# Shifting the queries by one position in a chunked gated linear attention with a feed-forward part

## The chip, the cores and the metric

One core of one Trainium2 chip runs the whole kernel. The metric is the device time of one execution in microseconds (us). The kernel before took 702.83 us in the median of 4 runs beside the changed kernel (702.4 to 703.86). All runs that are told here were of the fast state.

## The reference, cut to what matters

```python
# 4 batches, 8 heads, 768 tokens, head size 48; f = sigmoid(f_logit)
for t in range(S):
    state = f[:, :, t, :, None] * state + einsum('bhd,bhe->bhde', k[:, :, t], v[:, :, t])
    y[:, :, t] = einsum('bhd,bhde->bhe', q[:, :, t], state)
x = y.transpose(0, 2, 1, 3).reshape(3072, 384)
h = x @ w_in                                    # 384 -> 2048
out = (h * sigmoid(1.702 * h)) @ w_out          # 2048 -> 384
```

So a query at t sees its own key ungated, an older key at s through the gates s+1 to t, and whatever came before its chunk through the state.

## The kernel before

Everything is fp32; the weights arrive as 64-bit floats and are converted on VectorE in chains of integer and float operations, all in the first units. The tokens are cut into 12 units of 256 (three for each batch). Within a chunk of 64 tokens the attention is built from six levels: at level l, blocks of 2^l even keys meet the 2^l odd queries that follow them. After each level the odd halves of q and k are multiplied in place by the products of gates ("promote"), so that scores are always plain products. Units 0 to 2 run level by level ("fill"); units 3 to 11 run two levels in one stretch ("V"), and the matmuls of the feed-forward part of an earlier unit are put between the stretches in a fixed order.

```python
X = const.tile([P, 4, NA], F32, name="X")        # q, gated q, k, gated q of the other parity

def begin_q():                                   # gating of q
    nc.vector.tensor_tensor(X[:, J], X[:, 0], F, ALU.mult)

@part("W")
def _():                                         # level 0 and half of the diagonal: 128 columns
    order_v(n + 1)
    sc = scores()
    score(sc.rearrange("p h (a t) -> p h a t", a=NP), lambda h, x: X[rows(h), 2, x:x + G:2],
          lambda h, x: view(X, x, [[J * NA + 1, 2], [2, 64]])[rows(h)])
    promote(0)
    t["A"] = evacuate(512, [(0, 0)])             # scores x mask, 1024 wide

@part("W" if n < N_FILL else "V")
def _():                                         # odd keys x ungated odd queries, and level 1
    ...
    score(s4[:, 0], lambda h, x: X[rows(h), 2, x + 1:x + G:2], lambda h, x: X[rows(h), 0, x + 1:x + G:2])
    score(s4[:, 1], keys(1), tokens(J, LEV[1], 1))
    add(0, ..., start=True)                      # even values into all tokens: 128 columns
    promote(1, True); promote(2)
    t["A"] = evacuate(512, [(0, 0), (256, 1)])

def levels(l):                                   # two more stretches of two levels
    ...

# later: k transposed back (tkn), states st = st * gates + k v^T, then
py += st[c - 1] x X[J]                           # "inter": state of the chunk before x gated q
```

(Cut; `...` marks what is left out.) The tiles in the profile: sc is the PSUM tile of scores (also used for the sums k v^T), A the masked scores, y the PSUM output of the attention, Kc and Qc packed copies of even keys and odd queries, vl the values in the order of a level, st the states, tot the products of gates on GpSimd, bits, a and s the steps of the weights' conversion, h, sg, g and o the feed-forward part, yT and xT its input.

Of the kernel before, what the change touches and what calls it, by code (L numbers as in the profile page):

```python
# [13 lines left out]
ALU = mybir.AluOpType  # L14
# [9 lines left out]
def kernel(  # L24
# [9 lines left out]
):  # L34

# [82 lines left out]
    for u in range(2, NL + 1):  # L118
        nc.gpsimd.tensor_copy(
            perm[:, u - 2].rearrange("p (n m) -> p n m", m=LEV[u - 1]),  # L120
            ident.rearrange("p (n two m) -> p two n m", two=2, m=LEV[u - 1])[:, 0],
        )
# [3 lines left out]


    X = const.tile([P, 4, NA], F32, name="X")
# [107 lines left out]
    V_HALF = [(1, 0), (1, 1)] + [(m, 0) for m in LEV[1:]]  # L236
    NV = len(V_HALF)

# [32 lines left out]
    def load_vl(n, u):  # L271


        if n >= NALL:
            return
        if n < N_TURN:
            for i, x in enumerate((0, 1) if u == 0 else (u,)):
                pt = ps.tile([P, DM], F32, tag="mm", name=f"tv_{n}_{x}", bufs=4)
                for g in range(NG):
                    nc.tensor.matmul(  # L280
                        pt[g * 64:(g + 1) * 64], lhsT=ident[:, x::2] if u == 0 else perm[:, u - 2, :], rhs=vns[n][:, g, :],
                        start=True, stop=True,
                    )
                if i == 0:
                    t = ld.tile([P, 2, DM] if u == 0 else [P, DM], F32, tag=f"vl{u}", name=f"vl_{n}_{u}")
                vls[n, x] = t[:, x] if u == 0 else t
                nc.scalar.copy(vls[n, x], pt)
            return
        v_tok = v_toks[n % 2]
        if u == 0:  # L290
            t = ld.tile([P, 2, DM], F32, tag="vl0", name=f"vl_{n}_0")
            nc.sync.dma_start(out=t, in_=v_tok.rearrange("(p two) e -> p two e", two=2))
            vls[n, 0], vls[n, 1] = t[:, 0], t[:, 1]
        else:
            m, half = V_HALF[u]
            t = vls[n, u] = ld.tile([P, DM], F32, tag=f"vl{u}", name=f"vl_{n}_{u}")
            nc.sync.dma_start(out=t, in_=v_tok.rearrange("(n two m) e -> two n m e", two=2, m=m)[half])
# [22 lines left out]
    def attention(n):  # L320
# [4 lines left out]
        J = 1 if n < N_FILL or (n - N_FILL) % 2 else 3  # L325
        t = {}
# [32 lines left out]
        def begin():  # L359
            turn(1, X[:, 0])  # L360
            if n:
                load_raw(n + 1, 1)

        def begin_k():
            turn(2, X[:, 2])
            if n:
                load_raw(n + 1, 2)

        def begin_gates():
            t["tot"] = att.tile([P, NA], F32, tag="tot", name=f"tot_{n}")  # L370
            t["tms"], off = [F], 0
            for m in LEV:
                nb = NA // (2 * m)
                t2 = t["tms"][-1].rearrange("p (n two) -> p n two", two=2)
                tn = t["tot"][:, off:off + nb]
                nc.gpsimd.tensor_tensor(tn, t2[:, :, 0], t2[:, :, 1], ALU.mult)  # L376
                t["tms"].append(tn)
                off += nb

        def begin_q():  # L380
            nc.vector.tensor_tensor(X[:, J], X[:, 0], F, ALU.mult)
# [13 lines left out]
        def keys(l, tag="Kc"):  # L395
            return lambda h, x: t[tag, l][rows(h), x // 2:x // 2 + 64]
# [20 lines left out]

        def promote(l, q_too=False):

# [4 lines left out]
            qk = view(X, J * NA + m, [[(2 - J) * NA - m, 2], [2 * m, nb], [1, m]])  # L424
# [6 lines left out]
            if l + 1 < NL:  # L431
                m = LEV[l + 1]
                for tag, j, hf in (("Kc", 2, 0), ("Qc", J, 1))[:1 + q_too]:
                    c = t[tag, l + 1] = att.tile([P, NA // 2], F32, tag=tag, name=f"{tag}_{n}_{l}", bufs=2)
                    nc.scalar.copy(  # L435
                        c.rearrange("p (n m) -> p n m", m=m),
                        X[:, j].rearrange("p (n two m) -> p n two m", two=2, m=m)[:, :, hf, :],
                    )
# [17 lines left out]
        @part("W")  # L456
        def _():
            order_v(n + 1)
            sc = scores()
            score(  # L460
                sc.rearrange("p h (a t) -> p h a t", a=NP), lambda h, x: X[rows(h), 2, x:x + G:2],
                lambda h, x: view(X, x, [[J * NA + 1, 2], [2, 64]])[rows(h)],
            )
            promote(0)
            t["A"] = evacuate(512, [(0, 0)])

        @part("W" if n < N_FILL else "V")
        def _():
            sc = scores()
            s4 = sc.rearrange("p h (s a t) -> p s h a t", s=2, a=NP)  # L470
            score(s4[:, 0], lambda h, x: X[rows(h), 2, x + 1:x + G:2], lambda h, x: X[rows(h), 0, x + 1:x + G:2])
            score(s4[:, 1], keys(1), tokens(J, LEV[1], 1))
            A = t["A"]
            t["py"] = ps.tile([P, NG, NP, G], F32, tag="y", name=f"y_{n}")
            add(
                0, lambda h, g, a: A[g * 64:(g + 1) * 64, h, a * G:(a + 1) * G].rearrange("p (two n) -> p n two", two=2),
                lambda h, g, a: t["py"][columns(h, g), g, a, :], start=True,
            )
            if n < N_FILL:
                promote(1)  # L480
            else:
                promote(1, True)
                promote(2)
            t["A"] = evacuate(512, [(0, 0), (256, 1)])

        def level(l):
            sc = scores()
            score(sc[:, :, :256].rearrange("p h (a t) -> p h a t", a=NP), keys(l), tokens(J, LEV[l], 1))
            if l == 2:
                add(1, slot(t["A"], 0), half(1, 1))  # L490
                add(2, slot(t["A"], 256), half(LEV[1], 1))
            else:
                add(l, slot(t["A"], 0), half(LEV[l - 1], 1))
            if n + 1 >= N_TURN:
                for u in (0, 2) if l == 2 else (l,):
                    load_vl(n + 1, u)
            promote(l)
            t["A"] = evacuate(256, [(0, l)])

        def levels(l):  # L500
# [4 lines left out]
            for u, c in ((l - 1, 0), (l, 256)):  # L505
                add(u, slot(t["A"], c), half(LEV[max(u - 1, 0)], 1))
            for u in ((0, 2) if l == 2 else (l - 1, l)):
                load_vl(n + 1, u)
# [5 lines left out]
        if n < N_FILL:  # L514
            for l in range(2, NL):
                part("W")(lambda l=l: level(l))
        else:
            for l in range(2, NL, 2):
                part("V")(lambda l=l: levels(l))

        def turn_k(a0):
# [3 lines left out]
            for a in range(2):  # L525
                for g in range(NG):
                    x = (a0 + a) * U + g * G
                    nc.tensor.transpose(pt[:, a, g, :], X[:, 2, x:x + G], ident)  # L528
# [6 lines left out]
        def _():  # L535
            if n >= N_FILL:
                add(NL - 1, slot(t["A"], 0), half(LEV[-2], 1))
                load_vl(n + 1, NL - 1)
            add(NL, slot(t["A"], 0 if n < N_FILL else 256), half(LEV[-1], 1))
            if n + 1 >= N_TURN:  # L540
                load_vl(n + 1, NL)
# [17 lines left out]
            prev = last.get("st")  # L559
# [13 lines left out]
        def _():  # L573
# [4 lines left out]
            for cs in ((1, 2), (3, 0)):  # L578
                for a in range(NP):
                    for c in cs:  # L580
                        if t["before"][c] is None:
                            continue
                        for h in range(2):
                            x = a * U + c * C
                            nc.tensor.matmul(  # L585
                                py[columns(h, c // 2), c // 2, a, c % 2 * C:(c % 2 + 1) * C],
                                lhsT=t["before"][c][rows(h), a], rhs=X[rows(h), J, x:x + C],
                                start=False, stop=True, skip_group_check=True,
                            )
            yT = att.tile([P, NP, NG, G], F32, tag="kn", name=f"yT_{n}", bufs=1)  # L590
            xT = xTs[n] = mlp.tile([P, NK, U], F32, tag="xT", name=f"xT_{n}", bufs=3)
            for g in range(NG):
                for h in range(2):
                    nc.scalar.copy(yT[rows(h), :, g, :], py[columns(h, g), g])  # L594
            for h in range(2):
                nc.sync.dma_start(
                    out=xT[h * D:(h + 1) * D].rearrange("p c (g t) -> p c g t", g=NG), in_=yT[rows(h), :NK]
                )
                at = 0
                while at < D:  # L600
# [3 lines left out]
                        out=xT[D2 + p:D2 + p + w, c].rearrange("p (g t) -> p g t", g=NG),  # L604
                        in_=yT[h * HS + at:h * HS + at + w, NK],
# [3 lines left out]
        return (begin_f, begin, begin_k, begin_gates, begin_q), parts  # L609


    xTs = {}

    def mlp_h(n, ffs, g):
        t = {}

        def one(ff, c):
            if c == 0:
                if ff % FG == 0:
                    g[ff // FG] = mlp.tile([P, FG, U], F32, tag="g", name=f"g_{n}_{ff}", bufs=6)  # L620
                t["ph"] = ps.tile([P, U], F32, tag="mm", name=f"h_{n}_{ff}", bufs=4)
# [4 lines left out]
            if c == NK - 1:  # L626
                sg = mlp.tile([P, U], F32, tag="sg", name=f"sg_{n}_{ff}")
                nc.scalar.activation(sg, ph, AF.Sigmoid, scale=1.702)  # L628
                nc.vector.tensor_tensor(g[ff // FG][:, ff % FG, :], ph, sg, ALU.mult)  # L629
        return [(U, lambda ff=ff, c=c: one(ff, c), ff // FG * NPC + ff % FG + 1) for ff in ffs for c in range(NK)]  # L630
# [16 lines left out]
    def store(n, tt, o):  # L647
        r0 = n * U + tt * P
# [168 lines left out]
```

## Time and profile before

| | before |
|---|---|
| median, 4 runs | 702.83 us |
| span of the profiled run | 699.6 us |
| TensorE (PE) busy | 677.3 us |
| VectorE (DVE) busy | 397.6 us |
| granted clock, 40 to 60 us | 0.83 (1.00 in the other stretches) |
| period of a steady unit (start of one inter group to the next) | 53.33 us |

The prediction below shows the page's busy shares, the TensorE groups by shape, and a steady unit. One more view is needed for the comparison: what TensorE waited for in the kernel before (who waited for whom: us in all, times, longest).

```profile
PE sc L387 <- DVE A L411: 6.6, 4, 3.1
PE t L346 <- DMA raw<-in_f_logit_dram: 4.4, 1, 4.4
PE o L639 <- DVE g L629: 2.3, 1, 2.3
```

Of the 22 us that TensorE is idle in the whole span, 17.5 are waits in the first 100 us, most of them for VectorE; 1.3 lie between 120 and 220 us, and 3.5 are the end, after the last matmul. So, as an estimate from these waits, a TensorE instruction that goes is worth its whole distance to the next one after about 100 us, and nothing where TensorE stands waiting for VectorE anyway.

### The profile page before, as it was taken

Reading aid. Unit: us, or ns where it says so; the run is one execution under the profiler, and the core shown is the slowest. Engines: PE = TensorE matmul, PEld = TensorE weight load, DVE = VectorE, ACT = ScalarE, POOL = GpSimd, SP = SyncE. Lnnn points to the kernel's source line nnn. Section 1 sums busy time; section 2 is a strip of 40 time slices with the busy share of each in tenths; the row PEclk is TensorE's granted clock in tenths of the full one; section 3 lists DMA queues with packets and bytes.
Section 4 is the critical chain, followed back from the end, with each engine's and each line's share of the span. In section 5 each row is a group of like instructions: output and inputs, shape, how many; then the busy total and the mean of one; then the engine's idle time right before and its main releaser. Section 6 shows DMA issues by size and latency. Waiting matters only on the chain.

```text
span 699.6 us, 20710 instructions
## 1 busy us (share of the span) xinstructions
PE 677.3 (97%) x9208; PEld 507.4 (73%) x9208; DVE 397.6 (57%) x683; ACT 211.7 (30%) x440; POOL 40.6 (6%) x90
## 2 busy tenths in 40 slices
PE   6869989999999999999999999999999999999998
PEld 5647767767776876786786786786786786786774
DVE  4998787986767644644744744744644644441120
ACT  4544433233213322322322322322322332231110
POOL 3020100010002001001001001001001001000000
PEclk9998999999999999999999999999999999999999
DMA  8867963581063615406405405405504202101000
GB/s 205 213 174 185 226 165 103 149 186 37 23 154 102 154 46 144 116 23 151 130 23 145 135 25 144 135 24 138 142 24 113 60 23 65 29 2 36 11 1 22
DMA packets 66898, 69.67 MB, mean 100 GB/s; under 512 B 29944, under 2 KB 59256, under 8 KB 66808
## 3 DMA queue, kind: packets, MB, share of 16 engines
q1 hardware_dynamic: 66808, 68.34, 38.2%
q8 instruction: 72, 1.18, 0.7%
q14 instruction: 18, 0.15, 0.1%
HBM read 58.88 MB, written 8.65 MB: 97 GB/s over the span
## 4 chain that ended last, share of the span: by engine, by line
PE 89%; DVE 6%; DMA 2%; SPq 1%; issue 1%; ACT 1%; DVEq 0%; ACTq 0%
PE o L639 36%; PE h L623 35%; PE sc L387 7%; PE y L445 6%; PE y L585 2%; DMA bits<-in_moe_w_in_dram 1%; PE sc L549 1%; PE tkn L528 1%; DVE s L211 1%; DVE A L411 1%; SPq L246 1%; DVE a L219 1%; DVE X L428 1%; PE t L346 1%; DMA raw<-in_q_dram 1%
## 5 line engine op out<-in xcount | busy, mean ns | idle before, releaser
L623 PE MATMUL h<-xT,w_in 128*128 128x256 f32 x1152 | 262.7, 383 | 0.8 <-DVE g L629 0.8
L639 PE MATMUL o<-w_out,g 128*128 128x384 f32 x768 | 260.7, 491 | 2.3 <-DVE g L629 2.3
L623 PEld LDWEIGHTS h<-xT,w_in 128*128 128x128 f32 x1152 | 216.2, 191 | 36.2 <-issue 2.2
L639 PEld LDWEIGHTS o<-w_out,g 128*128 128x128 f32 x768 | 142.4, 190 | 96.0 <-issue 5.0
L629 DVE TENSOR_TENSOR g<-h,sg 128x256 f32<-128x256 f32 x192 | 80.3, 423 | 143.0 <-ACT sg L628 142.8
L628 ACT ACTIVATE sg<-h 128x256 f32<-128x256 f32 x192 | 72.7, 383 | 177.4 <-PE h L623 167.5
L435 ACT COPY Kc<-X 128x512 f32<-128x512 f32 x60 | 37.7, 629 | 115.0 <-DVE X L430 85.0
L430 DVE TENSOR_TENSOR X<-X,tot 128x1024 f32<-128x1024 f32 x45 | 55.0, 1222 | 19.6 <-PE sc L387 16.2
L411 DVE TENSOR_TENSOR A<-sc,masks 128x512 f32<-128x512 f32 (+1 forms) x84 | 61.1, 756 | 0.0
L445 PE MATMUL y<-A,vl 64*48 64x64 f32 (+1 forms) x2688 | 56.8, 230 | 0.6 <-issue 0.5
L445 PEld LDWEIGHTS y<-A,vl 64*48 64x48 f32 x2688 | 48.9, 121 | 6.1 <-issue 5.8
L334 DVE STREAM_TRANSPOSE X<-raw 128x1024 f32<-128x1024 f32 x18 | 36.9, 2048 | 20.4 <-PE sc L387 14.1
L376 POOL TENSOR_TENSOR tot<-F 128x512 f32<-128x512 f32 x12 | 12.5, 1040 | 544.3 <-DVE st L566 487.5
L658 ACT COPY osb<-o 128x384 f32<-128x384 f32 x18 | 8.6, 478 | 108.8 <-PE o L639 108.7
L594 ACT COPY yT<-y 48x512 f32<-48x512 f32 x48 | 27.8, 580 | 16.6 <-PE y L585 16.0
L387 PE MATMUL sc<-X,Kc 48*64 48x64 f32 x1344 | 28.3, 222 | 2.5 <-DVE A L411 2.5
L387 PEld LDWEIGHTS sc<-X,Kc 48*64 48x64 f32 x1344 | 24.2, 136 | 7.2 <-issue 3.2
L387 PEld LDWEIGHTS sc<-X 48*64 48x64 f32 x768 | 18.6, 138 | 13.8 <-issue 9.3
L569 DVE TENSOR_TENSOR st<-st,sc 128x192 f32<-128x192 f32 x44 | 15.6, 354 | 22.6 <-PE sc L549 21.2
L387 PE MATMUL sc<-X 48*64 48x128 f32 (+1 forms) x768 | 22.9, 254 | 5.5 <-DVE A L411 4.2
L566 DVE TENSOR_TENSOR st<-st,tot 128x192 f32<-128x192 f32 x44 | 15.7, 357 | 20.8 <-PE y L585 11.9
L376 POOL TENSOR_TENSOR tot<-tot 128x256 f32<-128x256 f32 (+4 forms) x60 | 25.8, 431 | 4.7
(52 smaller groups left out, 383.2 us busy)
## 6 DMA issues: line engine op xcount, KB each, us to landing
vl<-v_tok SPq DMA_DIRECT2D x50, 192.0 KB, 2.9
bits<-in_moe_w_out_dram SPq DMA_DIRECT2D x8, 768.0 KB, 8.2
bits<-in_moe_w_in_dram SPq DMA_DIRECT2D x8, 576.0 KB, 7.6
v_tok<-in_v_dram SPq DMA_DIRECT2D x10, 384.0 KB, 6.3
vl<-v_tok SPq DMA_DIRECT2D x10, 384.0 KB
vn<-v_tok SPq DMA_DIRECT2D x10, 384.0 KB, 6.0
xT<-yT SPq DMA_DIRECT2D x24, 144.0 KB, 2.6
raw<-in_f_logit_dram SPq DMA_DIRECT2D x18, 192.0 KB, 4.3
```

What stands on the lines that cost most here:

```text
L334: nc.vector.transpose(out.rearrange("p (a i j) -> p a j i", a=NP, j=R), raw[:, j].rearrange("p a (j d) -> p (a j) d", j=R)[:, :, :32],)
L376: nc.gpsimd.tensor_tensor(tn, t2[:, :, 0], t2[:, :, 1], ALU.mult)
L387: nc.tensor.matmul(out[g * HS:(g + 1) * HS, h, a, :], lhsT=lhs(h, a * U + g * G), rhs=rhs(h, a * U + g * G), start=True, stop=True,)
L411: nc.vector.tensor_tensor(A[:, :, c:c + w].rearrange("p h (x t) -> p h x t", t=64), t["sc"][:, :, c:c + w].rearrange("p h (x t) -> p h x t ...
L430: nc.vector.tensor_tensor(qk, qk, by, ALU.mult)
L435: nc.scalar.copy(c.rearrange("p (n m) -> p n m", m=m), X[:, j].rearrange("p (n two m) -> p n two m", two=2, m=m)[:, :, hf, :],)
L445: nc.tensor.matmul(dst(h, g, a), lhsT=vls[n, u][g * 64:(g + 1) * 64, (2 * a + h) * D:(2 * a + h + 1) * D], rhs=A(h, g, a), start=(start an ...
L594: nc.scalar.copy(yT[rows(h), :, g, :], py[columns(h, g), g])
L623: nc.tensor.matmul(ph, lhsT=w_in[:, c, ff * P:(ff + 1) * P], rhs=xTs[n][:, c, :], start=(c == 0), stop=(c == NK - 1))
L628: nc.scalar.activation(sg, ph, AF.Sigmoid, scale=1.702)
L629: nc.vector.tensor_tensor(g[ff // FG][:, ff % FG, :], ph, sg, ALU.mult)
L639: nc.tensor.matmul(t["po"], lhsT=g[ff // FG][:, ff % FG, tt * P:(tt + 1) * P], rhs=w_out[:, ff, :], start=(ff == ffs[0]), stop=(ff == ffs[ ...
```

## The change

Its intent: q is written one position later in its row. Then the gates that an older key must pass to reach the query (those up to and including t) are just the gates that stand before the query's new place, and no query shares its place with its own key: the diagonal falls away, with its scores, its values and the gated copy of q. The own key of a query comes through the state or an ordinary level. In return the last query of each unit comes to stand at the first place of the next unit (two small copies), where it needs the state of the unit that it came from; where the next unit begins a batch, that takes one-column inter matmuls, which it had no need of before. The very last token comes out alone at the end.

```diff
-    X = const.tile([P, 4, NA], F32, name="X")
+    NX = NA + 1
+    X = const.tile([P, 3, NX], F32, name="X")
+    q_last = {-1: const.tile([P, NP], F32, name="q_none")}
         def begin():
-            turn(1, X[:, 0])
+            turn(1, X[:, J, 1:])
+            q_last[n] = att.tile([P, NP], F32, tag="q_last", name=f"q_last_{n}", bufs=2)
+            nc.gpsimd.tensor_copy(q_last[n], view(X, J * NX + U, [[U, NP]]))
+            nc.gpsimd.tensor_copy(view(X, J * NX, [[U, NP]]), q_last[n - 1])
         def begin_k():
-            turn(2, X[:, 2])
+            turn(2, X[:, 1, :NA])
+            if n >= N_FILL:
+                set_aside(0, True)      # copies Kc, Qc of level 0 on ScalarE
+                promote(0)
-        def begin_q():
-            nc.vector.tensor_tensor(X[:, J], X[:, 0], F, ALU.mult)
-        (the part with 128 columns, and the part with the ungated odd diagonal)
+        (level 0 is one of six equal levels of 64 columns)
-            for l in range(2, NL, 2):
+            for l in range(0, NL, 2):
                 part("V")(lambda l=l: levels(l))
-                        if t["before"][c] is None:
-                            continue
+                        w = C if t["before"][c] is not None else 1
+                        ...             # w columns with the state of the unit before
-        r0 = n * U + tt * P
+        r0 = n * U + tt * P - 1
+        (the last token: y_last, 257 columns of h in the last unit, sum_last on VectorE, o_last)
```

(Cut to its core. Besides, the inter matmuls of every unit now stand in the first part of the next one, where before this held from unit 3 on, and the conversions of units 0 and 1 are spread over 26 shares instead of 29.)

## The prediction

> **What bounds the kernel now.** I read the page's busy shares and slices first, then the PE groups by shape, then the PE timeline of one steady unit, then the PE and DVE timelines of the start. TensorE is the bound almost everywhere:
>
> ```profile
> PE 677.3 (97%) x9208; PEld 507.4 (73%) x9208; DVE 397.6 (57%) x683; ACT 211.7 (30%) x440; POOL 40.6 (6%) x90
> ...
> PE   6869989999999999999999999999999999999998
> ...
> DVE  4998787986767644644744744744644644441120
> ...
> PE 89%; DVE 6%; DMA 2%; SPq 1%; issue 1%; ACT 1%; DVEq 0%; ACTq 0%
> ```
>
> The reader should see 22 us of idle PE in a 699.6 us span, nearly all in the first 100 us. Stretches of 20 us give PE 82.5 busy of the first 100 (13.3, 16.5, 15.2, 20.0, 17.5), and 20.0 of 20 from 220 us until the last stretch. DVE is 20.0 of 20 busy in 20 to 40 us and 18.1 in 40 to 60. So there are two regimes: a start set by DVE (unit 0 and half of unit 1; DVE also converts the weights there), and then PE alone, with the matmuls of the feed-forward part (h, o) filling every gap of the attention.
>
> The attention's matmuls by shape. Each matmul is two records in the trace: a group that the program issues as 16 shows as x32.
>
> ```profile
> L445 PE MATMUL y<-A,vl 64*48 64x64 f32 x2304 | 40.6, 217 | 0.6 <-issue 0.5
> L387 PE MATMUL sc<-X,Kc 48*64 48x64 f32 x1344 | 28.3, 222 | 2.5 <-DVE A L411 2.5
> L445 PE MATMUL y<-A,vl 64*48 64x128 f32 x384 | 16.2, 307 | 0.0
> L387 PE MATMUL sc<-X 48*64 48x128 f32 x384 | 14.0, 276 | 1.4 <-ACT X L349 0.7 <-DVE X L381 0.7
> L387 PE MATMUL sc<-Qc,Kc 48*64 48x64 f32 x576 | 12.5, 224 | 0.0
> L387 PE MATMUL sc<-X 48*64 48x64 f32 x384 | 9.0, 232 | 4.2 <-DVE A L411 4.2
> ```
>
> The two 128-column groups are the diagonal's packaging: even keys against gated even and odd queries, and even values into all tokens. A steady unit (period 53.3 us) shows what they cost in place. What I read from these lines is the distance from a start to the next start; the durations overlap.
>
> ```profile
> 429.71 1.11 PE L585 MATMUL y<-X,st 48*48 48x64 f32 x64
> 430.64 1.10 PE L387 MATMUL sc<-X 48*64 48x128 f32 x32
> 431.67 6.07 PE L639 MATMUL o<-w_out,g 128*128 128x384 f32 x18
> 437.67 0.72 PE L387 MATMUL sc<-X 48*64 48x64 f32 x32
> 438.21 0.66 PE L387 MATMUL sc<-X,Kc 48*64 48x64 f32 x32
> 438.68 1.28 PE L445 MATMUL y<-A,vl 64*48 64x128 f32 x32
> 439.89 4.78 PE L639 MATMUL o<-w_out,g 128*128 128x384 f32 x14
> ...
> 447.62 0.69 PE L387 MATMUL sc<-Qc,Kc 48*64 48x64 f32 x32
> 448.14 0.65 PE L387 MATMUL sc<-X,Kc 48*64 48x64 f32 x32
> 448.61 1.07 PE L445 MATMUL y<-A,vl 64*48 64x64 f32 x64
> 449.61 7.61 PE L623 MATMUL h<-xT,w_in 128*128 128x256 f32 x34
> ```
>
> No line has an idle mark. Finally the DVE timeline where unit 1 begins; its X L381 is the gating of q:
>
> ```profile
> 42.83 1.93 DVE L381 TENSOR_TENSOR X<-X,F 128x1024 f32<-128x1024 f32 x1
> ...
> 48.63 1.21 DVE L411 TENSOR_TENSOR A<-sc,masks 128x1024 f32<-128x1024 f32 x1
> ```
>
> DVE is busy without a gap from 12.9 to 55 us, and PE stands idle 3.13 us, to 49.98, for that A.
>
> [...] The change adds one-column matmuls, and nothing here shows any; I cost them like 64-column ones. [...] The trace has 1222 for the promotes of X and 1217 for the wide eviction[...]. [...] The new rows of X are 1025 long, so q and k start at odd words; I assume no cost. [...] after the 3.13 us gap the 64-column score group took 1.13 us instead of 0.72, and the stretch from 40 to 60 us has a granted clock of 0.83. Some 2.6 us were lost there (score groups about 0.4 each, the y group 0.65, the h group 3.21 against 1.99).
>
> **The change part by part.**
> Scores. Before, a unit has one 128-column group, one ungated 64-column group and five levels of 64. After: six levels of 64. So the 64-column groups stay at six (2304 records before and after) and the 128-column one goes: 14.0 us of busy PE in 12 units. In place, a steady unit pays 1.03 (430.64 to 431.67) + 1.01 (437.67 to 438.68) + 2 x 0.99 = 4.02 us and will pay 3 x 0.99 = 2.97: minus 1.05.
> Values. The 128-column group goes, six 64-column groups stay: 16.2 us busy. In place: 1.21 us a unit (438.68 to 439.89).
> So 2.26 us a steady unit by distances (30.2/12 = 2.52 by busy time; I take the smaller, as group edges overlap). Nine steady units: 9 x 2.26 = 20.3 us, all on the path, as PE never idles there.
> DVE, steady: gating q (1.36 us) and the wide eviction (1.22) go. Worth nothing there; DVE was at 8 to 14 of 20.
> ACT, steady: two more copies a unit (Kc, Qc of level 0), 0.62 each. ACT is at 4 to 7 of 20: hidden. They stand before promote 0, which now follows the transposition of k in the previous unit: 2.05 + 0.65 + 1.22 + 0.6 = 4.5 us from about 418.6 in that unit's time, while the first scores come at 430.6. About 7 us to spare.
> GpSimd: two 128x4 copies a unit, long before their use: hidden.
> Start, to the A of unit 1 (49.85 us). The instruction order puts the same number of conversions ahead of this A, so on a DVE without gaps the saving is what DVE loses: gating of unit 1 1.93; the 1024-wide evictions become 512-wide, 1.22 to 0.68 twice, 1.08; and one 0.6 eviction fewer in unit 0. Sum 3.6. Unit 0's gating (at 10.66, DVE waiting for ACT afterwards anyway) gives nothing, and neither does PE work removed there (scores, values, and a sixth of the matmuls that reorder values in units 0 and 1, 8 records of 0.22 = 1.8 us).
> Rest of unit 1 and first scores of unit 2 (to 98 us). PE work removed: 0.54 + 0.65 + 0.55 = 1.7. The 2.27 us wait of PE at 95 (for g, behind unit 2's gating, conversions and wide eviction) should shrink by 1.2 + 0.5. The clock loss of 2.6 may go[...]. Against it: conversions are spread over 26 shares instead of 29, so 5 operations (2.5 us of DVE) come earlier in unit 1, where DVE has little room. I take 3.5.
> Rest of unit 2: 0.54 + 0.65 = 1.2.
> Added. One-column matmuls on units 0, 3, 6, 9: 16 records each, a quarter of a 64-record group of 0.93 to 1.1 us, 0.25 to 0.3 us; three of them in the PE-bound part: 0.9. The last token: one more column in 48 h matmuls, 48 x 1.8 ns (0.456 us for 256 columns) = 0.1; one extra 384-column matmul of two records at 0.34: 0.7. Its 16 DVE operations (about 0.56 each, plus g at 0.42) make 1.0 us per h group of 3 x 0.456 = 1.37 us: hidden. Its small transfers have 25 o matmuls, 17 us, before the first h that needs them: hidden.
> Sum: -20.3 - 3.6 - 3.5 - 1.2 + 0.9 + 0.8 = -26.9. Predicted: 702.5 - 26.9 = 675.6 us, a ratio of 0.962.
>
> **The rivals.**
> (a) A new wait takes the gain: promote 0 of the next unit now hangs on ACT copies, and DVE and ACT work in order, so evictions and g behind it could hold PE up once a unit. For it: with one stretch fewer, all waits have less cover. Against it: the fill between stretches grows (13 to 14 o-sized matmuls, about 9 us, instead of 9 to 11.7), and a stretch needs DVE for 2 x 1.22 + 2 x 0.68 = 3.8. One wait of 1 us a unit would make 685.
> (b) The start is bound by something that the change doesn't touch: the weights' transfers (DMA at 0.72 to 0.88 until 100 us). For it: ACT waited 2.0 us for them at 19.1. Against it: DVE was behind them all the time. Then the start gives 3 instead of 7 us: 680.
> (c) The start gives more: PE work, idle and clock recovered in full, and 2.52 a unit. Then 20.3 becomes 22.7 and 7.1 becomes 10: 670.
> (d) Unaligned rows cost PE or DVE reads something: 5% on promotes and transposes would be hidden on DVE; on the k transposes (0.86 us a unit) below 1 us in all.
>
> **Range and chances.** The steady term is read from distances in place and should hold to 2 us; the start to 3 or 4; (a) is unlikely but costs most. Range 671 to 681. Faster by over 2% (below 688.4) needs only two thirds of the steady term plus little of the start: 0.96. Within 2%: 0.03. Slower: 0.01.
>
> **What would show it.** Period of a steady unit 51.0 instead of 53.3, no idle of PE after 220 us; no 128-column group in y or sc; PE busy near 647 (677.3 - 14.0 - 16.2 - 1.8 + 1.7). The A of unit 1's first level near 46.3 us; clock of 40 to 60 us nearer 1. One-column matmuls at 0.3 us a unit. The prediction is wrong if the steady period falls by less than 2 us, if PE shows idle before first scores, or if the first 100 us come out less than 4 or more than 11 us earlier.

## The result, and the profile after

The changed kernel took 678.23 us in the median of 4 runs (675.73 to 679.34), 24.6 us less. The ratio is 0.9643, with a 95% interval of 0.9613 to 0.9673. A ratio here is the mean time of one kernel's fast runs over that of the other's of the same rounds, so it isn't quite the ratio of the medians.

The page of the changed kernel (span 674.0 us), the same rows as before:

```profile
PE 652.6 (97%) x8514; PEld 486.5 (72%) x8514; DVE 378.4 (56%) x675; ACT 226.4 (34%) x459; POOL 50.3 (7%) x116
...
PE   5879999999999999999999999999999999999997
...
PE 89%; DVE 7%; ACT 2%; issue 1%; DMA 1%; SPq 0%; DVEq 0%; ACTq 0%
```

The span fell by 25.6 us and TensorE's busy time by 24.7: its idle time, 22.3 us before, is still 21.4. The gain is TensorE work that is gone, hardly any waiting that is gone. The groups by shape (line, engine, operation, tile, shapes, count, then busy us and mean ns) show which work:

```profile
L447 PE MATMUL y<-A,vl 64*48 64x64 f32 x2304 | 41.7, 219 | 0.0
L383 PE MATMUL sc<-X,Kc 48*64 48x64 f32 x1344 | 29.0, 224 | 6.8 <-ACT Kc L422 4.6 <-DVE A L409 2.1
L383 PE MATMUL sc<-Qc,Kc 48*64 48x64 f32 x864 | 18.6, 223 | 0.2 <-DVE st L542 0.2
L562 PE MATMUL y<-X,st 48*48 48x1 f32 x48 | 1.5, 180 | 0.0
```

No 128-column group is left; y keeps its 2304 records of 64 columns; new are the one-column ones. A steady unit of the changed kernel (start us, us, engine, line, what; an idle mark would stand at the end of a line):

```profile
412.34 1.11 PE L562 MATMUL y<-X,st 48*48 48x64 f32 x64
413.27 0.65 PE L383 MATMUL sc<-Qc,Kc 48*64 48x64 f32 x32
413.73 0.65 PE L383 MATMUL sc<-X,Kc 48*64 48x64 f32 x32
414.32 9.30 PE L645 MATMUL o<-w_out,g 128*128 128x384 f32 x28
423.54 0.70 PE L383 MATMUL sc<-Qc,Kc 48*64 48x64 f32 x32
424.06 0.65 PE L383 MATMUL sc<-X,Kc 48*64 48x64 f32 x32
424.53 1.08 PE L447 MATMUL y<-A,vl 64*48 64x64 f32 x64
425.53 1.56 PE L645 MATMUL o<-w_out,g 128*128 128x384 f32 x4
```

The first stretch is 1.05 us of scores (413.27 to 414.32) where before there were 1.03 for the 128-column group and then a stretch with another 1.01. The periods from unit 4 to 10 are 51.38, then six of 50.94 or 50.95; before they were 53.79, then 53.33 to 53.39. That is 2.39 us a unit less. What TensorE waited for:

```profile
PE sc L383 <- ACT Kc L422: 4.6, 2, 2.7
PE t L338 <- DMA raw<-in_f_logit_dram: 4.4, 1, 4.4
PE sc L383 <- DVE A L409: 2.1, 2, 1.6
```

All waits lie before 160 us. So the time splits well at the inter matmuls of unit 3, from where on the two traces of the changed kernel agree to 0.1 us:

| profiled runs | inter of unit 3 at | from there to the end |
|---|---|---|
| before | 215.9 us | 483.7 us |
| after | 208.1 us | 465.9 us |
| after, run again | 209.7 us | 465.8 us |

The later part gives 17.8 us. The start gives the rest of the 24.6 us between the medians, 6.8 (7.8 between the two profiled runs, 6.3 with the run again).

Now the start, where the prediction was less sure. VectorE at the first promotes of unit 1 (L435 and L436) and the scores' eviction after them:

```profile
44.95 0.91 DVE L435 TENSOR_TENSOR X<-X,F 128x512 f32<-128x512 f32 x1 [1.07 <-PE sc L383]
45.78 0.88 DVE L436 TENSOR_TENSOR X<-X,F 128x512 f32<-128x512 f32 x1
46.59 0.68 DVE L409 TENSOR_TENSOR A<-sc,masks 128x512 f32<-128x512 f32 x1
```

And TensorE's next scores, which wait until the copy of Kc has come out of ScalarE:

```profile
47.49 1.13 PE L383 MATMUL sc<-X,Kc 48*64 48x64 f32 x32 [2.67 <-ACT Kc L422]
```

The same scores began at 49.98 before. VectorE, without a gap there before, now has one of 1.07 us: it waits for scores that must first read q and k. The two promotes ran beside five products of GpSimd (2.91 us from 44.70 on) and took 0.91 and 0.88 us; in the kernel before they came after these products, at 47.42 and 48.02, and took 0.68 each. And a group that takes 0.69 us at full clock took 1.13 again, as before the change: the granted clock of 40 to 60 us is 0.83 in both kernels. (In this trace it is 0.83 from 20 to 40 us too, where the kernel before and the run again have 1.00.)

### The profile page after: what moved, and what is told of

Read it like the earlier page. It is cut to its first block, busy times and chain, and to the rows that moved or that the text cites. A ratio compares the mean times of both kernels' runs of the same rounds, so it can differ in the third digit from the quotient of the medians.

```text
span 674.0 us, 19354 instructions
## 1 busy us (share of the span) xinstructions
PE 652.6 (97%) x8514; PEld 486.5 (72%) x8514; DVE 378.4 (56%) x675; ACT 226.4 (34%) x459; POOL 50.3 (7%) x116
## 4 chain that ended last, share of the span: by engine, by line
PE 89%; DVE 7%; ACT 2%; issue 1%; DMA 1%; SPq 0%; DVEq 0%; ACTq 0%
PE h L619 37%; PE o L645 35%; PE sc L383 5%; PE y L447 5%; PE t L338 2%; PE y L562 2%; PE tkn L504 1%; PE sc L522 1%; DVE s L218 1%; DVE A L409 1%; DMA xT<-yT 1%; PE tv L283 1%; ACT yT L570 1%; DVE X L436 1%; DVE X L438 1%
## 5 line engine op out<-in xcount | busy, mean ns | idle before, releaser
L619 PE MATMUL h<-xT,w_in 128*128 128x256 f32 (+1 forms) x1152 | 261.1, 382 | 1.1 <-DVE sum L690 0.8
L625 DVE TENSOR_TENSOR g<-h,sg 128x256 f32<-128x256 f32 (+1 forms) x192 | 80.8, 422 | 133.1 <-ACT sg L624 132.6
L624 ACT ACTIVATE sg<-h 128x256 f32<-128x256 f32 (+1 forms) x192 | 73.2, 383 | 169.4 <-PE h L619 164.1
L422 ACT COPY Kc<-X 128x512 f32<-128x512 f32 x69 | 45.9, 666 | 123.7 <-DVE X L438 87.3
L438 DVE TENSOR_TENSOR X<-X,tot 128x1024 f32<-128x1024 f32 x45 | 55.2, 1226 | 54.8 <-PE sc L383 50.1
L409 DVE TENSOR_TENSOR A<-sc,masks 128x512 f32<-128x512 f32 x72 | 46.7, 679 | 0.0
L326 DVE STREAM_TRANSPOSE X<-raw 128x1024 f32<-128x1024 f32 x18 | 36.7, 2039 | 16.7 <-PE y L562 13.9
L447 PE MATMUL y<-A,vl 64*48 64x64 f32 x2304 | 41.7, 219 | 0.0
L447 PEld LDWEIGHTS y<-A,vl 64*48 64x48 f32 x2304 | 36.8, 122 | 5.3 <-issue 5.0
L383 PEld LDWEIGHTS sc<-X,Kc 48*64 48x64 f32 x1344 | 24.6, 138 | 13.8 <-ACT Kc L422 7.2
L331 ACT ACTIVATE F<-F 128x1024 f32<-128x1024 f32 x9 | 9.5, 1057 | 49.0 <-DVE F L326 49.0
L338 PE MATMUL t<-ident,raw 128*64 128x128 f32 x288 | 19.6, 298 | 4.4 <-DMA raw<-in_f_logit_dram 4.4
L338 PEld LDWEIGHTS t<-ident,raw 128*64 128x64 f32 x288 | 18.4, 153 | 7.0 <-issue 6.1
```

The lines of the kernel that those rows point to most:

```text
L326: nc.vector.transpose(out.rearrange("p (a i j) -> p a j i", a=NP, j=R), raw[:, j].rearrange("p a (j d) -> p (a j) d", j=R)[:, :, :32],)
L338: nc.tensor.matmul(pt[h * HS:(h + 1) * HS, jj, :], lhsT=by_pair[j][:, h, x:x + HS], rhs=ident, start=True, stop=True)
L383: nc.tensor.matmul(out[g * HS:(g + 1) * HS, h, a, :], lhsT=lhs(h, a * U + g * G), rhs=rhs(h, a * U + g * G), start=True, stop=True,)
L409: nc.vector.tensor_tensor(A[:, :, c:c + w].rearrange("p h (x t) -> p h x t", t=64), t["sc"][:, :, c:c + w].rearrange("p h (x t) -> p h x t ...
L422: nc.scalar.copy(c.rearrange("p (n m) -> p n m", m=m), X[:, j, :NA].rearrange("p (n two m) -> p n two m", two=2, m=m)[:, :, hf, :],)
L438: nc.vector.tensor_tensor(qk, qk, by, ALU.mult)
```

## The experiments

All twelve gave correct results. Medians are compared with the changed kernel run again on the same chip (677.5 us) or, in the last two groups, by the ratio to the kernel before.

### The changed kernel again

No edit.

> The changed kernel once more, unaltered, for its spread and a second trace. My theory (the steady part is set by TensorE alone, the spread of 675.7 to 679.3 us comes from the first 150 us, where VectorE, the transfers and the TensorE clock decide): the steady unit is again 50.9 us to 0.1, and whatever the span differs by is found before the inter matmuls of unit 3 (208.1 us in the first trace). Rival: the steady units themselves vary (a wait that sometimes opens behind the earlier promote): then the period differs by more than 0.2 us from unit to unit or TensorE idles after 220 us.

Measured: 677.5 us (4 runs, 676.44 to 679.38), ratio 0.9641 (0.9617 to 0.9665). Its period is 50.94 again, and unit 3 begins at 209.7 instead of 208.1. So at least the difference between these two profiled runs is made in the start (all eight runs of this kernel spread over 3.65 us), and only the period can tell a change of a few tenths.

The record names a part of that spread. In both traces TensorE stops in the middle of the inter matmuls of unit 0, and the profile names no cause ("issue"): for 0.26 us in the first (to 43.90) and 0.58 in the second (to 44.65). VectorE's gap ahead of the first promotes is 1.07 us in the first. Such gaps are, as far as the traces tell, waits for instructions. The fourteen traces hold 31 TensorE gaps of this kind over 0.15 us. 26 of them lie between 33 and 47 us and come after the same number of matmuls in every trace that has them, 598 for the first and 724 or 725 for the second; with weight loads and semaphore instructions counted, in the kernel before and the changed one, that is 1217 and 1473 or 1474, each 193 or 194 more than a multiple of 256. The DMA queue q8, which the page lists as "instruction", moved 72 packets of 16 KB in the kernel before and 67 in the changed one, for 18416 and 17028 matmuls and weight loads, so one for about 256; in the four gaps of these two traces TensorE goes on 1.24 to 1.39 us after such a packet has landed. Why a packet comes late just there was not tried.

### VectorE's gating operation put back

```diff
         def begin_gates():
+            nc.vector.tensor_tensor(pad, X[:, J, 1:], F, ALU.mult)
```

> Changed kernel plus one 128x1024 VectorE product per unit, standing where the gating of q stood (its result unused). TensorE theory: nothing in the nine steady units; only units 1 and 2 can pay, about 1.2 to 1.9 us each where VectorE is full, so +1 to +4 us in all. VectorE rival (the gain came from VectorE's removed gating and eviction): 12 x 1.25, so +11 to +15 us.

Measured: 681.14 us, ratio 0.9692, 3.6 us slower than the changed kernel. The periods are the same to 0.01 us (51.37, 50.95, 50.94); unit 3 begins at 213.1. So the gating operation costs nothing in the steady units and 3 to 4 us in the start: the large part of the gain isn't VectorE's. The rival, with 11 us or more, falls.

### The scores' 128-column group put back

```diff
+            if l == 0:
+                score(
+                    t["sc"].rearrange("p h (a t) -> p h a t", a=NP), keys(0), lambda h, x: X[rows(h), J, x:x + G],
+                )
             score(s4[:, 0], keys(l), keys(l, "Qc"))
```

The results are overwritten by the real scores, so the output stays right.

> Changed kernel plus one extra group of sixteen 128-column score matmuls at the start of each of the nine steady units (result overwritten by the real scores). TensorE theory: each costs its distance in place in the kernel before, 1.03 us, so +9.3 us (8.5 to 10.5). Rival (the removed groups ran beside other work or beside each other, and the gain came from having fewer stretches and fewer waits): +4 us or less.

Measured: 685.9 us, 8.4 us slower. The period rises to 51.85, by 0.91 us (one is 52.38, with a gap of 0.37 in it that is marked "issue"). In the trace:

```profile
419.55 1.09 PE L383 MATMUL sc<-X,Kc 48*64 48x128 f32 x32
420.43 0.67 PE L383 MATMUL sc<-Qc,Kc 48*64 48x64 f32 x32
```

From start to start 0.88 us, less than the 1.03 us that the group of the kernel before took in place. The median is a hair below the range of the first theory, and far above the rival's.

### The values' 128-column group put back

```diff
+            if l == 0 and n >= N_FILL:
+                A = t["A"]
+                add(
+                    0, lambda h, g, a: A[g * 64:(g + 1) * 64, h, a * 64:a * 64 + G],
+                    lambda h, g, a: t["py"][columns(h, g), g, a, :], start=True,
+                )
             add(l, slot(t["A"], c), half(LEV[l], 1), start=(l == 0))
```

> Changed kernel plus one extra group of sixteen 128-column value matmuls ahead of the value matmuls of level 0 in each of the nine steady units. TensorE theory: 1.21 us each in place, so +10.9 us (10 to 12). Rival as for the scores: +4 us or less. With the scores' group the two should add up to about 20 us, the steady part of the gain.

Measured: 688.99 us, 11.5 us slower, which is what was expected. But the trace shows that it isn't for the reason given. The undisturbed periods are 51.82, only 0.87 longer; the rest is in the start (unit 3 at 211.3) and in TensorE gaps of 1.2 and 0.75 us, each in the middle of a long run of small matmuls, which the profile marks "issue" like those told above. So the median agreed by chance, and the term was 0.87 a unit, not 1.21. That left the question why the old group was dearer.

### The same with the old access pattern

The values' group of the kernel before took neighbouring columns from A in turn out of two halves that lie 64 elements apart; the one above reads A contiguously.

```diff
-                    0, lambda h, g, a: A[g * 64:(g + 1) * 64, h, a * 64:a * 64 + G],
+                    0, lambda h, g, a: A[g * 64:(g + 1) * 64, h, a * G:(a + 1) * G].rearrange("p (two n) -> p n two", two=2),
```

> As values_back, but the extra value group reads its 128 columns in the order of the kernel before: even and odd positions interleaved, a step of 64 elements between neighbours. In values_back, whose columns are contiguous, the group added 0.87 us to an undisturbed steady period, against 1.21 us between its start and the next in the kernel before. If the step is what made the removed group dear, the period now grows by 1.05 to 1.2 us. If 1.21 was the change of array layout at the group's end, it stays at 0.87 to 0.9.

Measured: 690.16 us; the period is 52.04, 1.10 above the changed kernel and 0.23 above the contiguous version (the two gaps are there again, of 0.85 and 0.77 us). The two groups side by side, first contiguous, then with the step (each line includes the 64 records that were there anyhow, whose distance is 1.00):

```profile
432.64 1.95 PE L447 MATMUL y<-A,vl 64*48 64x128 f32 x96
434.52 1.56 PE L651 MATMUL o<-w_out,g 128*128 128x384 f32 x4
```

```profile
432.42 2.17 PE L447 MATMUL y<-A,vl 64*48 64x128 f32 x96
434.51 1.56 PE L651 MATMUL o<-w_out,g 128*128 128x384 f32 x4
```

1.88 us against 2.09, so 0.88 and 1.09 for the group alone. The step of the moving operand is a real part of what the old group cost. A step of 64 fp32 elements cost 0.21 us by these distances and 0.23 by the periods, on 0.88; why, no run shows.

### The scores with the old access pattern

```diff
+            if l == 0:
+                score(
+                    t["sc"].rearrange("p h (a t) -> p h a t", a=NP), lambda h, x: X[rows(h), 1, x:x + G:2],
+                    lambda h, x: view(X, J * NX + x, [[1, 2], [2, 64]])[rows(h)],
+                )
```

> As scores_back, but the extra score group reads queries and keys as the kernel before did: every second token, keys too. In scores_back the group added 0.91 us to an undisturbed steady period, against 1.03 in place before. If the step of two costs TensorE something: 0.96 to 1.05 us. If not: 0.91 again.

Measured: 685.53 us; the periods lie between 51.86 and 52.10, most of them 51.86 to 51.91, so 0.92 to 0.97 above the changed kernel, and hardly above the contiguous 0.91. So the second branch of the expectation came, or nearly: a step of two elements costs next to nothing here, 0.06 us at most. So the scores' group was worth 0.92, and the 1.03 read in place seems to hold something that isn't the group's own.

### Each stretch cut in two

If it isn't the group's own, it may be what comes with a stretch: TensorE goes over from 128-row matmuls to 64-row ones and back. Here the scores and the values of a stretch are set apart, with feed-forward matmuls between, and there is not one matmul more. The expectation counts three more stretches; there are only two, because the first stretch of a steady unit has no values (`adds` is not called for l = 0), and its second half holds no TensorE work.

```diff
             score(s4[:, 1], keys(l + 1), tokens(J, LEV[l + 1], 1))
+
+        def rest(l):
             if l == 0:
-                part("V")(lambda l=l: levels(l))
+                part("H")(lambda l=l: levels(l))
+                part("H")(lambda l=l: rest(l))
```

(and a share of 2 for each H where V had 4)

> Changed kernel with each of the three stretches of a steady unit cut in two, scores in one and values in the next with feed-forward matmuls between: the same matmuls, three more changes of array layout each way. The steady period fell by 2.39 us where the matmuls' own distances explain 2.2; I put the rest down to one stretch fewer. Then three more stretches cost 3 x 0.15 to 0.2, the period is 51.4 to 51.5, and the span grows by 4 to 5 us. If a change of layout costs nothing, the period stays 50.9 and the span within 1 us.

Measured: 685.59 us, 8.1 us slower. The period is 51.63, 0.69 longer with no idle TensorE in any steady unit. In the trace, o and h matmuls now stand between scores (up to 431.52) and values, and the same once more between 442.68 and 447.19:

```profile
431.52 1.56 PE L648 MATMUL o<-w_out,g 128*128 128x384 f32 x4
432.91 3.19 PE L622 MATMUL h<-xT,w_in 128*128 128x256 f32 x14
436.03 1.11 PE L447 MATMUL y<-A,vl 64*48 64x64 f32 x64
```

So an additional stretch, there and back, costs 0.69 / 2 = 0.35 us, twice the 0.15 to 0.2 expected; what happens in that time, the trace doesn't show. Nine units of 0.69 make 6.2 us. The remaining 2 us lie before the inter matmuls of unit 2 (142.9, against 141.1 in the run again), in units whose code the edit leaves alone: the profiled run has a TensorE gap of 2.23 us there, up to 46.87, at the place where the run again has one of 0.58. It comes after the same 725 matmuls as the others.

### Work on VectorE ahead of promote 0

The first rival of the prediction was a new wait: promote 0 of the next unit now hangs on ScalarE and VectorE. Four dummy products (128 x 1024, 1.22 us each) were put in front of it in every unit from 3 on.

```diff
             if n >= N_FILL:
+                for _ in range(4):
+                    nc.vector.tensor_tensor(pad, X[:, 1, :NA], F, ALU.mult)
                 set_aside(0, True)
                 promote(0)
```

> Changed kernel with four extra 128x1024 VectorE products (4.6 us) before the earlier promote of each steady unit, on the very chain that the change lengthened (transposition of k, promote of level 0, states). In the changed kernel's trace the states end at 408.5 and are needed at 412.3. My theory, that this chain has several us to spare: period 50.94 unchanged; only the entry into unit 3, where VectorE is full, pays 1 to 5 us. Rival, that the earlier promote stands close to the path: the period grows by 1 us or more, +9 us in all.

Measured: 686.9 us, 9.4 us slower; the expected 1 to 5 us were missed. But the periods are 51.38, 50.94, 50.95 as without the dummies: nearly 5 us more work on VectorE change nothing in a steady unit. All the loss lies before the inter matmuls of unit 3, which begin at 218.3. The dummies of unit 3 show where:

```profile
145.05 0.32 PE L566 MATMUL y<-X,st 48*48 48x64 f32 x4 [3.27 <-DVE st L546]
```

These states stood in VectorE's order behind the products (135.72 to 140.72) and the promote after them: their first operation begins at 144.19, though their matmuls end at 136.43. The dummies of unit 4 cost too, beside the last conversions: 0.79 us of waiting at 210 us and 1.38 at 213. So there is slack for four such products in every later unit and none where the fill units hand over to the steady ones: VectorE has little room there (15.9 of 20 us busy from 120 to 140 us and 16.4 from 140 to 160 in the changed kernel, with conversions still to do).

### Conversions spread over more parts, promote 0 of unit 3 later, and both

Three attempts to give the start its expected gain. The first gives the part S of units 0 and 1 a share of the conversions, so that fewer stand ahead of the promotes; the second moves promote 0 of unit 3 behind the states; the third is both.

```diff
-        converting = {"W": 3, "T": 3, "B": 1} if n < N_FILL - 1 else ...
+        converting = {"W": 3, "T": 3, "B": 1, "S": 3} if n < N_FILL - 1 else ...
```

> Changed kernel with the weights' conversions of units 0 and 1 spread over 29 shares again, as before the change (some 4 to 5 operations, 2 us of VectorE, move from ahead of the states of unit 0 to behind them). In the changed kernel's trace VectorE idles 1.07 us after these states, waiting for the first scores of unit 1. Theory: the moved operations fill that hole and the states come 2 us earlier, so unit 1's first level is 1 us earlier and the span 0.5 to 1.5 us shorter (unit 3's inter matmuls at 207.5 to 209 instead of 208.1 to 210.4 us). Rival: VectorE is full either way and nothing changes.

Measured: 680.82 us in 6 runs, ratio 0.9701 (0.9676 to 0.9725), 2.6 us above the changed kernel's first median: the theory behind it is wrong. The hole of 1.07 us is filled, but with conversions that take 3.4 us there (42.53 to 45.93). TensorE waits 8.2 us in all for A and the copies of Kc, instead of 6.7, and 2.0 for g instead of 0.9.

```diff
-            if n >= N_FILL:
+            if n > N_FILL:
                 set_aside(0, True)
                 promote(0)
         def begin_gates():
+            if n == N_FILL:
+                set_aside(0, True)
+                promote(0)
```

> Changed kernel with unit 3's promote of level 0 and its two copies moved behind the states of unit 2, for this unit alone. In the trace VectorE waits 1.29 us for the copy, then promotes (1.23), and unit 2's states end at 141.3 although their matmuls were done at 134.2; TensorE's inter matmuls run from 139.6 to 141.6 instead of taking 0.93 us. Theory: the earlier promote does cost at this one place where VectorE is full, 1 to 2 us: unit 3's inter matmuls at 207 to 208.5. Rival: the place is bound by the conversions and sums behind, and nothing changes.

Measured: 677.12 us in 5 runs, ratio 0.9634 (0.961 to 0.9657); unit 3 begins at 207.6. The interval overlaps that of the changed kernel (0.9617 to 0.9665): whether it is faster by half a microsecond or not at all, these runs can't say.

> Both of the edits above. If both are right, they add: span 2 to 3 us shorter than the changed kernel, a median of 675 to 676 us, and a version better than both. If neither, 677 to 678.5.

Measured: 679.31 us, ratio 0.967 (0.9647 to 0.9693). The two don't add up; a loss like the first edit's stays, though the interval touches that of the changed kernel.

### The first scores ahead of the inter matmuls in units 1 and 2

The last attempt goes at the gap of 1.07 us shown above.

```diff
-            parts[0] = kind, lambda: (ahead(), scores())
+            parts[0] = kind, lambda: (scores(), ahead()) if n < N_FILL else (ahead(), scores())
```

> The changed kernel, with one order turned round in units 1 and 2: the first scores of the unit are put ahead of the inter matmuls of the unit before (later units as they were). The theory of the start: in the changed kernel VectorE stood idle for 1.07 us in front of promote 0 of unit 1, waiting for those scores, and ScalarE's Kc copy stood behind the four yT copies (2.37 us); that is where the expected gain of the start went. It then expects no idle of VectorE at that place, the scores of level 1 of unit 1 about 1 us earlier (46.3 to 46.8 us instead of 47.5), and 676 to 677 us in the median, 0.5 to 1.5 us below the changed kernel; the period of the steady units stays 50.94. The rival, that something else sets the start (the conversions, the weights' transfers or PE's own gaps without a visible cause): the gap moves, the inter matmuls and what hangs on them come later by what the scores came earlier, and the time is the changed kernel's, 677.5 to 678.5, or above. Both are within the spread of the start, so the trace of the first 60 us decides, not the median alone.

Measured: 683.39 us in 6 runs, ratio 0.972 (0.9692 to 0.9748), some 5 us slower; the periods are 50.94. The theory's order of cause falls, and the trace tells why:

```profile
44.28 0.72 PE L383 MATMUL sc<-X 48*64 48x64 f32 x32 [2.07 <-DVE st L542]
```

```profile
45.14 0.97 DVE L435 TENSOR_TENSOR X<-X,F 128x512 f32<-128x512 f32 x1 [1.01 <-PE sc L383]
```

Though nothing but q and k goes into these scores, TensorE held them back until the last state was done: they are written to the PSUM tile sc, which the states are still read from. So the gap of VectorE is a round trip through a buffer: the last state frees sc, TensorE scores, and only then may the promotes change q and k in place. It was 1.07 us and is 1.01 with the order turned. What the edit did change is that y, and with it xT, came later: TensorE then waited 1.44 us for xT, VectorE stood idle for 4.20 us, and the granted clock of 40 to 60 us was 0.66 (in this run it was 0.87 before 40 us too, which the edit doesn't touch). That is what the rival had said.

No variant clearly beats the changed kernel.

## Why the prediction was right, and where it was off

The predicted 675.6 us lies 2.6 us below the median of 678.23, within its range of 671 to 681; the mechanism, TensorE work that lies on the path in every steady unit, is what the runs show. Against its own sum:

| term | predicted | measured |
|---|---|---|
| eight periods, unit 4 to the end | 8 x 2.26 = -18.1 | 8 x 2.39 = -19.1 |
| one-column matmuls | +0.9 | about 0 |
| last token | +0.8 | +1.3 |
| start, with unit 3's own stretches | -3.6 - 3.5 - 1.2 - 2.26 = -10.6 | -6.8 |
| sum | -27.0 (-26.9 unrounded) | -24.6 |

(Measured: -19.1 + 1.3 = -17.8, as seen from unit 3 to the end. The last of the eight periods fell by 3.04 us, because two records of o of 0.33 us each had moved behind it; it is counted like the others. The start is the difference of the medians less these 17.8.)

**The steady term** was nearly right, 2.26 against 2.39, but its two parts were wrong and made up for what was missing. Put back alone, the values' group costs 1.10 with its old access pattern (1.21 predicted) and the scores' group 0.92 (1.05 predicted). The difference, 0.11 and 0.13, is put down to the change to the neighbouring kind of matmul, a part of which the distance from start to start in place seems to have held. What the prediction left out is that the change also takes away one of the five stretches of small matmuls in a unit, worth 0.35. Together 1.10 + 0.92 + 0.35 = 2.37, so the three put back alone leave nothing of the 2.39 that the scatter of the periods doesn't cover. (A slip without consequence: the even queries in the scores' 128-column group were the ungated ones, only the odd were gated.)

**The wait as a rival** (a) didn't come in the steady units: no idle TensorE after 160 us, and four more wide VectorE operations leave the period as it is. At the entry to unit 3 it did come, as waits of 1.3 us for kn (0.7 before), 0.8 for a sum and 0.2 for the states. The rival (b), a start that gives less, came in part; its reason, the weights' transfers, wasn't tested. The rival (c) put the steady unit at 2.52, as far above the measured 2.39 as the prediction was below, and the start too high. The rival (d) is nothing: a promote takes 1226 ns on the odd rows against 1222 before, a transposition on VectorE 2039 against 2048, and four records of the k transpositions on TensorE take 0.43 or 0.44 us from start to start in both.

**The one-column matmuls** cost nothing that shows. Their records in the inter group are 180 ns long, against 219 of 64 columns. In the kernel before, the inter matmuls of a first unit had 48 records and those of another 64, and the span from their start over the next scores was 1.96 us in both; in the changed kernel, with 16 one-column records added to the 48, it is 1.98 against 1.98 (361.39 to 363.37, and 412.34 to 414.32). The missing quarter had saved no time before, so filling it costs none. The prediction had counted records; that is not what this span goes by. Why, no run tests.

**The last token** was 0.41 us for y_last, 0.73 for o_last and 0.14 for the 257th column of h (the last 96 records of h take 20.86 us from start to start of what follows, before 20.72). The prediction had the last two (0.7 and 0.1) but not y_last.

**The start** is the term that failed, by 3.8 us, and it is most of the distance to the median. That the gating operation is worth 3 to 4 us there holds (3.6 in the experiment). The step "on a DVE without gaps the saving is what DVE loses" failed: the scores after A came 2.49 us earlier (47.49 against 49.98), not 3.6, since VectorE got a gap of 1.07 us, for a round trip through the sc buffer that gating and conversions had covered before. (44 conversion operations stand ahead of this A in both kernels, as predicted; but before, 5 of them stood between the last state and the promotes, and now none. Of the 1.07 us, 0.26 are TensorE's gap marked "issue".) The step "the clock loss of 2.6 may go" failed too: the gap of TensorE shrank from 3.13 us to 2.67, and the granted clock of that stretch was 0.83 all the same, with 1.13 us for the same scores. The length of the last gap doesn't tell in these traces: a score group took 1.13 us after 0.43 us (run again, at 17.22) and 0.70 after 2.19 (run shares, at 17.46). What sets the clock, no run shows. The wait for g shrank from 2.3 us to 0.9, as predicted. The waits at the entry to unit 3 took 1.6 us back (1.3 + 0.8 + 0.2 less the 0.7 of before), and a wait of 0.6 us for g at 212 us went, so 1.0 net. The first and the last make 2.1 of the 3.8 (of 2.8 between the two profiled runs, whose start differs by 7.8); that the unrecovered clock is the rest was not tried alone.

**The busy time** of TensorE was predicted near 647 and is 652.6. That figure was taken by subtracting the groups' busy times, which overlap at their edges. By distances it would have been 9 x 2.26 + 3 x 1.19 + 1.8 - 1.7 = 24.0 less, so 653.3.

## What to carry to other kernels

On the bound engine here a group of small matmuls was worth its distance from start to start, but part of that distance belonged to going over to another kind of matmul (0.35 us for a stretch, there and back) and part to the access pattern (0.23 us of the values' 1.10): the cheapest check is to put the group back alone and read the period of a steady unit, not the median. Before the cost of an edit is divided by what it added, count that in the trace. Operations removed from an engine that is full only in a start-up stretch can give less than their sum (2.49 us of 3.6 here), because they had covered round trips between engines (1.07 us of idle VectorE here); ask what buffer or in-place update the next operation waits for when the filler is gone. Before a wait is attacked by turning instructions round, look whether the tile that they write is free at all: here TensorE waited 2.07 us for sc with the order turned.
